# Attention and Strassen FFN on one core: first loads split over two queues, the first keys rounded on VectorE, and the operands of the first product stage made in fewer parts

## Chip, cores and metric

The kernel runs on one core of a Trainium2 chip. The metric is the device time of one execution in microseconds, taken as the median of three runs. Engines are named as in the profile: PE (TensorE matmul), PEld (its weight load), DVE (VectorE), ACT (ScalarE), POOL (GpSimd), SP (SyncE, which issues all DMAs here).

## What is computed

```python
def _attn_ref(q, k, v):                   # 8 batches, 12 heads, 448 tokens, 64 per head
    scores = scale * np.matmul(q, k.transpose(0, 1, 3, 2)) - np.log(S)
    attn = 1.0 / (1.0 + np.exp(-scores))  # sigmoid, so no row sums
    return np.matmul(attn, v)

def _moe_ref(x, w_in, w_out):             # x: 3584 x 768, from the heads laid side by side
    h = x @ w_in                          # 768 x 2048
    g = np.maximum(0.01 * h, h)
    return g @ w_out                      # 2048 x 768
```

## The kernel before

**Numbers in two parts.** A float32 operand of a score or of a feed-forward product is split into a rounded part ("high": a copy to float32r) and the rest ("low": a subtraction). Each product is then three matmuls: high by high, high by low, low by high. For q and k `Pair.high` is a copy on ACT and `Pair.low` a subtraction on DVE, both of a tile of 128x896 (448 columns of q, 448 of k).

**Attention.** The 96 heads are 48 pairs, two heads in the two halves of the partitions. `Pair.scores(h)` makes two of the four key chunks: six matmuls into a tile of two PSUM banks (pool `s`, three such tiles in the first stage, two later) and one sigmoid on ACT. `Pair.attn_v(h)` multiplies by v, and `Pair.keep` copies the sum out of PSUM into an x tile. Pairs 0, 9, 10 and 11 use four chunks of 112 keys; the others share a last chunk of 64 with a neighbour.

**Feed-forward.** Both layers are Strassen products: seven products per block of weights (`ORDER = 0, 1, 4, 5, 3, 6, 2`), from sums of quarters of x and of w. `prep` turns the float64 weights into float32 sums on DVE (some 14 steps a block: `wd`, `ws`) and stores them to DRAM (`t`). `Weights.load/high/low` bring them back and split them; `advance(t)` issues these steps ahead of product t. `Operands` makes the seven x operands: `s3`, `sum1`, `sum2`, `sum4` are subtractions or additions on DVE, `high(n, a, b)` a copy on ACT and `low(n, a, b)` a subtraction on DVE for columns a to b of operand n.

**Order.** Everything is issued in program order on each engine. The program is a row of slots, one piece of PE work each; `later(k, f)` puts f ahead of the PE work k slots on. In the first stage (`q == 0`, twelve pairs j) the slots are `e{j}.0` scores(1) of pair j, `e{j}.1` scores(0) of pair j+1, `e{j}.2` and `e{j}.3` attn_v of pair j. The next stage begins with `e0.0` to `e0.3` for pair 12 and then mixes attention with products p0, p1, and so on (five, five, four after a pair). The table `PLAN_ALONE` says ahead of which slot of the first stage ("e10.1") or of the second ("ne0.0", "np0") an operand step stands: "h422" is high of operand 4, columns 2 to 2; "l302" low of operand 3, columns 0 to 2; "s1.." to "s4.." the sums. `next_parts(i)` places the split of pair i+2 (high one slot on, low two) and the load of pair i+4 (four slots on). `prepare()` takes 1.5 steps of `prep` after a slot that is not `busy`.

**Start.** SP issues q and k of pair 0 as two loads, pair 1, v of pairs 0 and 1, three loads of weights, and later pair 2, which waits until pair 0's tile is free (`raws` has two buffers). ACT loads its table, then rounds q, k and pair 1; DVE subtracts.

Of the kernel before, what the change touches and what calls it, by code (L numbers as in the profile page):

```python
# [10 lines left out]
F32R = mybir.dt.float32r  # L11
I32 = mybir.dt.int32
AF = mybir.ActivationFunctionType
# [3 lines left out]
P = 128  # L17
# [39 lines left out]
def attn_ffn_kernel(ctx: ExitStack, tc: tile.TileContext, qk, v, w_in, w_out, out):  # L57
# [11 lines left out]
    nc = tc.nc  # L69
    B = 8  # L70
    S = qk.shape[3]
# [16 lines left out]
    def pinned(issue):  # L88

        return lambda *args, **kw: tc.keep_in_program_order(issue(*args, **kw))  # L90

    mm, dma = pinned(nc.tensor.matmul), pinned(nc.sync.dma_start)
    copy, act = pinned(nc.scalar.copy), pinned(nc.scalar.activation)
    vec, vec_s, vec_st = (pinned(x) for x in (nc.vector.tensor_tensor, nc.vector.tensor_scalar, nc.vector.scalar_tensor_tensor))

    def sub(to, x, y):
        vec(out=to, in0=x, in1=y, op=ALU.subtract)
# [10 lines left out]
    def later(slots, *fns, first=False):  # L108

        chores.setdefault(now + slots, ([], []))[not first].extend(fns)  # L110

    def slot(work=None):
        nonlocal now
        for fns in chores.pop(now, ()):
            for fn in fns:
                fn()
        if work is not None:
            work()
        now += 1
# [6 lines left out]
    class Weights:  # L126
# [17 lines left out]
        def high(self):  # L144
            pool, tag, bufs = self.to
            t = pool.tile([P, 1 if tag == "t1" else 2, 2, HW], F32R, tag=tag, name=f"w{self.w}_{self.u}_{self.g}", bufs=bufs)
            self.t = t[:, :self.n]
            copy(out=self.t[:, :, 0], in_=self.x)

        def low(self):  # L150
            sub(self.t[:, :, 1], self.x, self.t[:, :, 0])
# [59 lines left out]
    ps = ExitStack()  # L211
# [14 lines left out]
    def shift(stack, name, size, side="left"):  # L226

        return stack.enter_context(tc.tile_pool(name=name, bufs=1, side=side)).tile([P, size // 4], F32, tag=name, name=name)
# [4 lines left out]
    warm = shift(ctx, "warm", 32, "right")  # L233
    xp, pp, raws, spl, at = (right.enter_context(tc.tile_pool(name=name, bufs=bufs, side="right")) for name, bufs in (
        ("xp", 5), ("pp", 3), ("raws", 2), ("spl", 2), ("at", 5)))
# [8 lines left out]
    todo = [(w, u) for w in range(2) for u in range(NU)]  # L244
# [58 lines left out]

    xs = {}

    class Pair:


# [3 lines left out]

        def load_qk(self):
            self.raw = raws.tile([P, 2, S], F32, tag="qk", name=f"qk_{self.i}")
            for x in self.pieces():
                dma(out=self.raw[:, x], in_=qk[self.i, :, x])

        def load_v(self):
            rows, n = ((KR, 2 * NK), (P, 2 * NK - 2), (P, 2 * NK))[self.part]
            self.v = raws.tile([P, 2 * NK, D], F32, tag="v", name=f"v_{self.i}", bufs=2)  # L320
            dma(out=self.v[:rows, :n], in_=v[self.i, :rows, :n])

        def pieces(self):

            return (slice(0, 1), slice(1, 2)) if self.i == 0 else (slice(0, 2),)

        def high(self):
            self.parts = spl.tile([P, 2, 2, S], F32R, tag="qks", name=f"qks_{self.i}")
            for x in self.pieces():
                copy(out=self.parts[:, 0, x], in_=self.raw[:, x])  # L330

        def low(self):
            for x in self.pieces():
                sub(self.parts[:, 1, x], self.raw[:, x], self.parts[:, 0, x])

        def scores(self, h):
            for c in range(2 * h, 2 * h + 2):
                ps = psum("s", f"sc_{self.i}_{c}")

                if self.part == 0:  # L340
                    k0, n, rows = c * KR, KR, slice(0, KR)
                elif c < NK - 1:
                    k0, n, rows = c * P, P, slice(0, P)
                elif self.part == 1:
                    k0, n, rows = S - D, D, slice(0, D)
                else:
                    k0, n, rows = S - P, P, slice(D, P)
                for m, (kp, qp) in enumerate(((0, 0), (0, 1), (1, 0))):
                    for j, me in enumerate(heads):
                        mm(ps[:n, j, :S], lhsT=self.parts[me, kp, 1, k0:k0 + n], rhs=self.parts[me, qp, 0],  # L350
                           start=m == 0, stop=m == 2)
                if self.part == 2 and c == NK - 1:
                    s = pairs[self.i - 1].a[c]
                else:
                    s = at.tile([P, 2, S], F32, tag="s", name=f"s_{self.i}_{c}")
                act(out=s[rows], in_=ps[rows, :, :S], func=AF.Sigmoid, bias=bias, scale=scale)
                self.a.append(s)
# [27 lines left out]
    class Operands:  # L385
# [52 lines left out]
    PLAN_ALONE = {  # L438
# [4 lines left out]


    w1 = []
# [7 lines left out]
    def advance(t):  # L453

        nonlocal at_load, at_high, at_low
        while at_high < len(w1) and w1[at_high][0] <= t + 3:
            w1[at_high][1].high()
            at_high += 1
        while at_low < len(w1) and w1[at_low][0] <= t + 2:
            w1[at_low][1].low()  # L460
            at_low += 1
        while at_load < len(w1) and w1[at_load][0] <= t + 8 and at_load < at_low + len(w1_stage):
            x = w1[at_load][1]
            x.stage = w1_stage[-1]
            x.load()
            at_load += 1
# [61 lines left out]
    per = 2 * NP  # L528
    last = B * NP - 1
    pairs = [Pair(i) for i in range(B * NP)]  # L530
    nc.gpsimd.memset(warm, 0.0)
    act(out=warm, in_=warm, func=AF.Sigmoid)
    pairs[0].load_qk()
    pairs[1].load_qk()
    for i in range(2):
        pairs[i].load_v()
    next(preps)
    for i in range(2):
        pairs[i].high()
        pairs[i].low()  # L540
        pairs[i + 2].load_qk()
    first, ops = None, None
    psum = banks("ps_a", dict(s=(3, 2), pv=(2, 1)))

    def next_parts(i):
        if i + 2 <= last:
            later(1, pairs[i + 2].high)
            later(2, pairs[i + 2].low)
        if i + 4 <= last:
            later(4, pairs[i + 4].load_qk)  # L550

    def go(q, where, work, busy=False):

# [9 lines left out]
    for q in range(NQ + 1):  # L563
        before, ops = ops, Operands(q) if q < NQ else None
        if q == 0:
            slot(lambda: pairs[0].scores(0))
        elif q == 1:
            ps.close()
            psum = banks("ps_b", dict(s=(2, 2), pv=(2, 1), px=(1, 1), pz=(1, 1)))
        k = 0  # L570
        for j in range(per if q < NQ else 1):
            i = q * per + j
            if q == 0 and 0 < j:
                later(0, pairs[i + 1].load_v)
            if q == 0:
                busy = j >= per - 2
                go(q, f"e{j}.0", lambda: pairs[i].scores(1), busy)
                next_parts(i)
                if j + 1 < per:
                    go(q, f"e{j}.1", lambda: pairs[i + 1].scores(0), busy)  # L580
                    for h in range(2):
                        go(q, f"e{j}.{2 + h}", lambda: pairs[i].attn_v(h), busy)
                if j >= per - 4:
                    for t in range(2):
                        advance(2 * (j - per) + t)
                continue
            if j == 0:
                first = First(q - 1, before)
            busy = j == 0 or j == per - 1 or q == NQ
            go(q, f"e{j}.0", (lambda: pairs[i].scores(0)) if q < NQ else None, busy)  # L590
            for h in range(2):
                go(q, f"e{j}.{1 + h}", lambda: pairs[i - 1].attn_v(h), busy)
            go(q, f"e{j}.3", (lambda: pairs[i].scores(1)) if q < NQ else None, busy)
            if q < NQ:
                next_parts(i)
                if i < last:
                    later(1, pairs[i + 1].load_v)
                for _ in range(PRODUCTS[j % len(PRODUCTS)]):
                    go(q, f"p{k}", first.step, busy or j == per - 2 and k >= 50 or k < 7)
                    k += 1  # L600
# [39 lines left out]
    for k in range(NOP, NU * NOP):  # L640
        m, at = divmod(k - NOP, 6)
        if m < AHEAD:
            x = w2[use[m]]
# [22 lines left out]
    for i, (g, u) in enumerate(use[AHEAD:]):  # L666
        one = len(GROUPS[g]) == 1
        pool, tag = (ring, "ring") if i < len(GROUPS) else (t2b, "t1" if one else "t2")
# [85 lines left out]
```

## Time and profile before

| what | value |
|---|---|
| median of 3 runs | 1109.43 us (1107.17 to 1110.66) |
| the profiled execution | 1107.88 us |
| its span, first to last instruction | 1106.1 us |
| PE busy in the span | 1094.2 us (99%) |
| DVE busy, ACT busy | 651.4 us (59%), 617.6 us (56%) |
| DMA, mean over the span | 226 GB/s |

A row of the timeline gives start (us from the span's start), length (us), engine, line, operation, output<-input, shapes, and in brackets the idle time of the engine before it and what ended that. Rows of equal instructions are merged (x18). All helpers record at line 90, so rows are told apart by tile: `sc` scores, `s` sigmoids, `qk` the loaded q and k, `qks` their two parts, `so` operand parts, `x` attention outputs, `wx` and `w` weights loaded and split, `px`, `py`, `pz` PSUM of products, `c_h` their sums. In the order of a built program the names carry numbers: `qks_2` is pair 2, `s_11_3` chunk 3 of pair 11, `so4_0` operand 4 of the first product stage.

### The profile page before, as it was taken

Reading aid. Unit: us, or ns where it says so; the run is one execution under the profiler, and the core shown is the slowest. Engines: PE = TensorE matmul, PEld = TensorE weight load, DVE = VectorE, ACT = ScalarE, POOL = GpSimd, SP = SyncE. Lnnn points to the kernel's source line nnn. Section 1 sums busy time; section 2 is a strip of 40 time slices with the busy share of each in tenths; the row PEclk is TensorE's granted clock in tenths of the full one; section 3 lists DMA queues with packets and bytes.
Section 4 is the critical chain, followed back from the end, with each engine's and each line's share of the span. In section 5 each row is a group of like instructions: output and inputs, shape, how many; then the busy total and the mean of one; then the engine's idle time right before and its main releaser. Section 6 shows DMA issues by size and latency. Waiting matters only on the chain.

```text
span 1106.1 us, 15810 instructions
## 1 busy us (share of the span) xinstructions
PE 1094.2 (99%) x5952; PEld 895.1 (81%) x5952; DVE 651.4 (59%) x886; ACT 617.6 (56%) x883; POOL 0.3 (0%) x5
## 2 busy tenths in 40 slices
PE   8999999999999999999999999999999999999998
PEld 4547777777777777777777999999999999999998
DVE  5978777677666677666648666665433333343332
ACT  6897665677666668666667555554333233323331
POOL 0000000000000000000000000000000000000000
PEclk9999999999999999999999999999999999999999
DMA  8975888875878776788745889786655554454442
GB/s 289 326 249 189 311 284 284 310 254 185 264 273 289 275 234 211 242 274 292 242 151 177 264 270 297 268 280 214 206 147 150 158 175 150 133 177 150 156 149 93
DMA packets 101436, 250.08 MB, mean 226 GB/s; under 512 B 11280, under 2 KB 53904, under 8 KB 101360
## 3 DMA queue, kind: packets, MB, share of 16 engines
q1 hardware_dynamic: 101360, 249.08, 68.3%
q8 instruction: 46, 0.75, 0.3%
q14 instruction: 30, 0.25, 0.1%
HBM read 164.63 MB, written 84.41 MB: 225 GB/s over the span
## 4 chain that ended last, share of the span: by engine, by line
PE 95%; ACT 2%; DMA 1%; DVE 1%; issue 0%; SPq 0%; ACTq 0%
PE px_o L90 21%; PE px_h L90 21%; PE pv L90 11%; PE pz_h L90 11%; PE sc L90 11%; PE pz_o L90 10%; PE py_o L90 5%; PE py_h L90 5%; ACT s L90 1%; ACT so L90 1%; DMA v<-in_v 1%; DMA qk<-in_qk 0%; ACT qks L90 0%; DVE wd L90 0%; DVE so L90 0%
## 5 line engine op out<-in xcount | busy, mean ns | idle before, releaser
L90 DVE TENSOR_TENSOR gs<-gg,gs 128x896 fp32r<-128x896 f32 x112 | 122.4, 1092 | 226.8 <-ACT gs L90 226.7
L90 PE MATMUL px_h<-so,w 128*128 128x448 f32 x1152 | 249.7, 363 | 0.2 <-ACT c_h L90 0.2
L90 PE MATMUL px_o<-gs,w 128*128 128x448 f32 x1152 | 232.5, 362 | 0.0
L90 PEld LDWEIGHTS px_h<-so,w 128*128 128x128 f32 x1152 | 214.8, 187 | 19.7 <-issue 3.0
L90 ACT CAST gs<-gg 128x896 fp32r<-128x896 f32 x112 | 105.6, 943 | 221.7 <-PE px_o L90 116.1
L90 PEld LDWEIGHTS px_o<-gs,w 128*128 128x128 f32 x1152 | 216.0, 187 | 14.4
L90 ACT ACTIVATE s<-sc 128x896 f32<-128x896 f32 (+1 forms) x192 | 171.5, 917 | 59.4 <-PE sc L90 35.0
L90 PE MATMUL sc<-qks 64*128 64x448 f32 (+2 forms) x1152 | 144.7, 386 | 8.0 <-ACT qks L90 4.6
L90 DVE TENSOR_TENSOR w<-wx,w 128x768 fp32r<-128x768 f32 (+1 forms) x160 | 136.1, 853 | 26.8 <-ACT w L90 26.3
L90 PEld LDWEIGHTS sc<-qks 64*128 64x128 f32 (+2 forms) x1152 | 98.3, 180 | 65.5 <-issue 28.2
L90 PE MATMUL pv<-s,v 128*64 128x448 f32 (+2 forms) x768 | 144.1, 551 | 0.2 <-DMA v<-in_v 0.2
L90 PE MATMUL pz_h<-so,w 128*128 128x448 f32 x576 | 128.3, 367 | 0.0
L90 ACT CAST w<-wx 128x768 fp32r<-128x768 f32 (+1 forms) x160 | 119.9, 753 | 6.2 <-DMA wx<-t 6.1
L90 PEld LDWEIGHTS pz_h<-so,w 128*128 128x128 f32 x576 | 106.2, 188 | 14.8 <-issue 7.0
L90 PE MATMUL pz_o<-gs,w 128*128 128x448 f32 x576 | 116.5, 362 | 0.0
L90 PEld LDWEIGHTS pz_o<-gs,w 128*128 128x128 f32 x576 | 108.0, 187 | 7.2
L90 PEld LDWEIGHTS pv<-s,v 128*64 128x64 f32 (+2 forms) x768 | 44.0, 136 | 78.3 <-issue 77.4
L90 ACT COPY c_h<-px_h 128x448 f32<-128x448 f32 x64 | 34.1, 533 | 68.6 <-PE px_h L90 68.5
L90 PE MATMUL py_h<-so,w 128*128 128x448 f32 x288 | 62.8, 362 | 0.0
L90 DVE TENSOR_TENSOR qks<-qk,qks 128x896 fp32r<-128x896 f32 (+1 forms) x49 | 52.3, 1068 | 17.1 <-ACT qks L90 16.9
L90 DVE SCALAR_TENSOR_TENSOR wd<-wr,wd 128x768 int32<-128x768 int32 x64 | 61.2, 956 | 1.1
L90 ACT ACTIVATE c_h<-c_h 128x448 f32<-128x448 f32 x96 | 55.4, 577 | 10.1 <-DVE c_h L90 9.8
(37 smaller groups left out, 660.8 us busy)
## 6 DMA issues: line engine op xcount, KB each, us to landing
gg<-g SPq DMA_DIRECT2D x112, 448.0 KB, 3.5
wx<-t SPq DMA_DIRECT2D x120, 384.0 KB, 3.9
g<-c_h SPq DMA_DIRECT2D x128, 224.0 KB, 4.4
g<-s SPq DMA_DIRECT2D x96, 224.0 KB, 4.4
qk<-in_qk SPq DMA_DIRECT2D x47, 448.0 KB, 4.9
wr<-in_w_in SPq DMA_DIRECT2D x16, 768.0 KB, 7.1
t<-ws SPq DMA_DIRECT2D x16, 768.0 KB, 7.1
wr<-in_w_out SPq DMA_DIRECT2D x16, 768.0 KB, 5.9
```

Of the source, the lines that this page charges most:

```text
L90: return lambda *args, **kw: tc.keep_in_program_order(issue(*args, **kw))
```

## The change

The first loads: q of pair 0 goes out on ACT's queue, its k in two halves of 224 columns on SP's, and of the weights none until pair 0 is split. Pair 0 is split in a new function: ACT rounds q, DVE rounds each half of the keys and subtracts; pair 1 is rounded on DVE. The first two score chunks are issued term by term, not chunk by chunk. In the first stage q and k of pair i+2 are split one slot sooner (high ahead of `e{j}.1`, low ahead of `e{j}.2`, the load three slots on). Weights of product 0 on are loaded and split two pairs sooner. `PLAN_ALONE` makes operands 1 (as before), 3, 6, 2 and the sums `s1`, `s4` whole, and from np0 on. The slots of j = 0 are now `busy`, so `prep` starts one pair later.

```diff
@@ Pair
         def load_qk(self):
             self.raw = raws.tile([P, 2, S], F32, tag="qk", name=f"qk_{self.i}")
-            for x in self.pieces():
-                dma(out=self.raw[:, x], in_=qk[self.i, :, x])
+            if self.i == 0:
+                dma_act(out=self.raw[:, 0], in_=qk[self.i, :, 0])
+                for cols in KEYS:
+                    dma(out=self.raw[:, 1, cols], in_=qk[self.i, :, 1, cols])
+            else:
+                dma(out=self.raw, in_=qk[self.i])
...
+        def split(self):
+            self.parts = spl.tile([P, 2, 2, S], F32R, tag="qks", name=f"qks_{self.i}")
+            high, low = self.parts[:, 0], self.parts[:, 1]
+            copy(out=high[:, 0], in_=self.raw[:, 0])
+            vcopy(out=high[:, 1, KEYS[0]], in_=self.raw[:, 1, KEYS[0]])
+            sub(low[:, 0], self.raw[:, 0], high[:, 0])
+            for n, cols in enumerate(KEYS):
+                if n > 0:
+                    vcopy(out=high[:, 1, cols], in_=self.raw[:, 1, cols])
+                sub(low[:, 1, cols], self.raw[:, 1, cols], high[:, 1, cols])
@@ PLAN_ALONE
-        "e10.1": "s200", "e10.2": "h400 s100", "e10.3": "l400 h300", "e11.0": "l300 h600",
-        "ne0.0": "s211 h411 l600", "ne0.1": "l411 s111", "ne0.2": "s401", "ne0.3": "s222",
-        "np0": "h422 l422", "np1": "s122 h312 h201", "np2": "l312 h612", "np3": "l612 s422", "np4": "l201 h222", "np5": "l222"}
+        "e10.1": "s200", "e10.2": "h400", "e10.3": "l400", "ne0.0": "s211 h411", "ne0.1": "l411", "ne0.3": "s222",
+        "np0": "h422 l422 s102", "np1": "h302", "np2": "l302 h602", "np3": "l602 s402", "np4": "h202", "np5": "l202"}
@@ the first stage
-    act(out=warm, in_=warm, func=AF.Sigmoid)
     pairs[0].load_qk()
     pairs[1].load_qk()
-    for i in range(2):
-        pairs[i].load_v()
+    pairs[0].load_v()
+    act(out=warm, in_=warm, func=AF.Sigmoid)
+    pairs[0].split()
+    pairs[2].load_qk()
     next(preps)
-    for i in range(2):
-        pairs[i].high()
-        pairs[i].low()
-        pairs[i + 2].load_qk()
+    pairs[1].high(vcopy)
+    pairs[1].low()
+    pairs[3].load_qk()
...
-                busy = j >= per - 2
+                busy = j == 0 or j >= per - 2
                 go(q, f"e{j}.0", lambda: pairs[i].scores(1), busy)
-                next_parts(i)
+                next_parts(i, 0, 1, 3)
...
-                if j >= per - 4:
+                if per - 6 <= j < per - 2:
                     for t in range(2):
-                        advance(2 * (j - per) + t)
+                        advance(2 * (j - per + 2) + t)
```

The order of SP at the start, before:

```order
L90 DMA qk_0_138<-in_qk 128x448 x2
L90 DMA qk_1_141<-in_qk 128x896
L90 DMA v_0_143<-in_v 112x512
L90 DMA v_1_145<-in_v 128x384
L90 DMA wr0_0_0_147<-in_w_in 128x1536
L90 DMA wr0_0_1_149<-in_w_in 128x1536
L90 DMA wr0_1_0_203<-in_w_in 128x1536
L90 DMA qk_2_156<-in_qk 128x896
```

and now (`wr` are raw weights):

```order
L90 DMA qk_0_137<-in_qk 128x224 x2
L90 DMA qk_1_141<-in_qk 128x896
L90 DMA v_0_143<-in_v 112x512
L90 DMA v_1_185<-in_v 128x384
L90 DMA qk_2_153<-in_qk 128x896
L90 DMA wr0_0_0_155<-in_w_in 128x1536
L90 DMA wr0_0_1_157<-in_w_in 128x1536
L90 DMA qk_3_162<-in_qk 128x896
```

Pair 2 now stands ahead of all weights, and q of pair 0 is no longer on this queue.

The order of ACT at the end of the first stage, from the second sigmoid of pair 11 to the last, before:

```order
L90 ACTIVATE s_11_1_850<-sc_11_1_843 112x896
L90 CAST qks_12_852<-qk_12_768 128x896
L90 CAST so4_0_854<-s2_0_832 128x448
L90 CAST so3_0_864<-x_2_617 128x448
L90 CAST w0_0_0_872<-wx0_0_0_741 128x2x384
L90 COPY x_3_808<-pv_10_857 128x448
L90 CAST so6_0_878<-x_3_808 128x448
L90 ACTIVATE s_11_2_887<-sc_11_2_880 112x896
L90 ACTIVATE s_11_3_896<-sc_11_3_889 112x896
```

and now:

```order
L90 CAST qks_12_839<-qk_12_746 128x896
L90 ACTIVATE s_11_0_851<-sc_11_0_843 112x896
L90 ACTIVATE s_11_1_859<-sc_11_1_844 112x896
L90 CAST so4_0_862<-s2_0_841 128x448
L90 COPY x_3_815<-pv_10_864 128x448
L90 ACTIVATE s_11_2_887<-sc_11_2_879 112x896
L90 ACTIVATE s_11_3_895<-sc_11_3_880 112x896
```

Between the second and the third sigmoid of pair 11 six instructions stood on ACT, and now two.

The order of DVE from the last piece of operand 4 on, around products p0 to p3, before:

```order
L90 TENSOR_TENSOR so4_0_854<-s2_0_832,so4_0_854 128x448
L90 TENSOR_TENSOR w0_0_1_901<-wx0_0_1_806,w0_0_1_901 128x2x384
L90 TENSOR_TENSOR x_2_617<-x_2_617,x_3_808 128x448
L90 TENSOR_TENSOR c11_h0_0_982<-c11_h0_0_982,py_h0_0_994 128x448
L90 TENSOR_TENSOR qks_14_984<-qk_14_907,qks_14_984 128x896
L90 TENSOR_TENSOR so3_0_864<-x_2_617,so3_0_864 128x896
L90 TENSOR_TENSOR w0_0_2_992<-wx0_0_2_870,w0_0_2_992 128x2x384
L90 TENSOR_TENSOR so6_0_878<-x_3_808,so6_0_878 128x896
L90 TENSOR_TENSOR x_1_494<-x_1_494,s2_0_832 128x448
```

and now:

```order
L90 TENSOR_TENSOR so4_0_862<-s2_0_841,so4_0_862 128x448
L90 TENSOR_TENSOR x_2_614<-x_2_614,x_3_815 128x1344
L90 TENSOR_TENSOR w0_0_1_813<-wx0_0_1_677,w0_0_1_813 128x2x384
L90 TENSOR_TENSOR c11_h0_0_972<-c11_h0_0_972,py_h0_0_982 128x448
L90 TENSOR_TENSOR qks_14_974<-qk_14_875,qks_14_974 128x896
L90 TENSOR_TENSOR so3_0_978<-x_2_614,so3_0_978 128x1344
L90 TENSOR_TENSOR w0_0_2_980<-wx0_0_2_740,w0_0_2_980 128x2x384
L90 TENSOR_TENSOR so6_0_995<-x_3_815,so6_0_995 128x1344
L90 TENSOR_TENSOR x_1_485<-x_1_485,s2_0_841 128x1344
```

The sum into `x_2` is now whole and stands ahead of the weights of product p2, and the three passes behind it are whole too. On ACT the high part of operand 2, which reads `x_1`, stands ahead of the weights of the next block and of the sigmoids of pair 13.

## Rows read from the trace of the kernel before

**Rows 1.** All that PE waited for, whole span (us in total, times, longest).

```profile
PE sc L90 <- ACT qks L90: 4.6, 1, 4.6
PE sc L90 <- ACT s L90: 2.4, 2, 1.8
PE sc L90 <- DVE qks L90: 0.9, 2, 0.7
PE pv L90 <- DMA v<-in_v: 0.2, 1, 0.2
PE px_h L90 <- ACT c_h L90: 0.2, 1, 0.2
```

**Rows 2.** Timeline of PE, first 17 us: start us, us, and idle before in brackets.

```profile
4.59 3.70 PE L90 MATMUL sc<-qks 64*112 64x448 f32 x18 [4.59 <-ACT qks L90]
8.94 3.70 PE L90 MATMUL sc<-qks 64*112 64x448 f32 x18 [0.64 <-ACT s L90]
12.57 3.62 PE L90 MATMUL pv<-s,v 112*64 112x448 f32 x16
16.12 2.82 PE L90 MATMUL sc<-qks 64*128 64x448 f32 x24
```

**Rows 3.** Stretch of the first matmuls: length, PE, PEld, DVE, ACT, POOL busy, granted clock, DMA.

```profile
4.59:8.29 3.70, 3.69 (x18) 2.51 (x18) 0.80 (x2) 1.16 (x2) 0.00 (x0) 1.00 1.01 340
```

**Rows 4.** Timeline of ACT, first 8 us.

```profile
3.19 0.56 ACT L90 CAST qks<-qk 128x448 fp32r<-128x448 f32 x1 [0.95 <-DMA qk<-in_qk]
...
3.98 0.57 ACT L90 CAST qks<-qk 128x448 fp32r<-128x448 f32 x1 [0.23 <-DMA qk<-in_qk]
...
7.13 0.94 ACT L90 CAST qks<-qk 128x896 fp32r<-128x896 f32 x1 [2.58 <-DMA qk<-in_qk]
7.97 3.38 ACT L90 ACTIVATE s<-sc 112x896 f32<-112x896 f32 x4
```

**Rows 5.** Groups by shape, 0 to 95 us: busy us, mean ns of one | idle before.

```profile
L90 DVE TENSOR_TENSOR qks<-qk,qks 128x896 fp32r<-128x896 f32 x14 | 15.3, 1091 | 13.2 <-ACT qks L90 13.0
...
L90 DVE TENSOR_SCALAR wd<-wr 128x768 int32<-128x768 int32 x9 | 5.0, 555 | 0.9 <-DMA wr<-in_w_in 0.9
L90 DVE TENSOR_TENSOR so<-x,so 128x1344 fp32r<-128x1344 f32 x3 | 4.7, 1557 | 0.8 <-ACT so L90 0.7
...
L90 ACT CAST so<-x 128x1344 fp32r<-128x1344 f32 x3 | 3.9, 1311 | 0.0
...
L90 DVE TENSOR_TENSOR w<-wx,w 128x768 fp32r<-128x768 f32 x3 | 2.9, 952 | 0.0
```

**Rows 6.** Timeline of ACT, a split whose other part comes late.

```profile
56.08 0.94 ACT L90 CAST qks<-qk 128x896 fp32r<-128x896 f32 x1
```

**Rows 7.** Timeline of PE, 58 to 98 us.

```profile
58.20 1.27 PE L90 MATMUL sc<-qks 64*112 64x448 f32 x10 [0.66 <-DVE qks L90]
...
74.78 2.11 PE L90 MATMUL sc<-qks 64*112 64x448 f32 x18
78.68 0.87 PE L90 MATMUL sc<-qks 64*128 64x448 f32 x6 [1.80 <-ACT s L90]
...
84.06 2.08 PE L90 MATMUL px_h<-so,w 128*128 128x448 f32 x9
...
87.77 1.96 PE L90 MATMUL px_h<-so,w 128*128 128x448 f32 x9
...
97.55 1.49 PE L90 MATMUL sc<-qks 64*128 64x448 f32 x12
```

**Rows 8.** Timeline of ACT ahead of the longest wait in Rows 7.

```profile
74.34 0.57 ACT L90 CAST so<-s 128x448 fp32r<-128x448 f32 x1
...
76.01 0.53 ACT L90 COPY x<-pv 128x448 f32<-128x448 f32 x1
...
76.90 1.73 ACT L90 ACTIVATE s<-sc 112x896 f32<-112x896 f32 x2
```

**Rows 9.** Timeline of DVE, the last piece of operand 4.

```profile
85.82 0.62 DVE L90 TENSOR_TENSOR so<-s,so 128x448 fp32r<-128x448 f32 x1 [0.84 <-ACT so L90]
```

More of the change, by code (lines that the diff above doesn't have):

```diff
@@ L92, in attn_ffn_kernel @@
     mm, dma = pinned(nc.tensor.matmul), pinned(nc.sync.dma_start)
-    copy, act = pinned(nc.scalar.copy), pinned(nc.scalar.activation)
+    copy, act, dma_act = (pinned(x) for x in (nc.scalar.copy, nc.scalar.activation, nc.scalar.dma_start))
+    vcopy = pinned(nc.vector.tensor_copy)
     vec, vec_s, vec_st = (pinned(x) for x in (nc.vector.tensor_tensor, nc.vector.tensor_scalar, nc.vector.scalar_tensor_tensor))
@@ L304, in attn_ffn_kernel @@
     xs = {}
+    KEYS = slice(0, S // 2), slice(S // 2, S)
     class Pair:
@@ L321, in load_v, with high @@
             dma(out=self.v[:rows, :n], in_=v[self.i, :rows, :n])
-        def pieces(self):
-            return (slice(0, 1), slice(1, 2)) if self.i == 0 else (slice(0, 2),)
-        def high(self):
+        def high(self, how=None):
             self.parts = spl.tile([P, 2, 2, S], F32R, tag="qks", name=f"qks_{self.i}")
-            for x in self.pieces():
-                copy(out=self.parts[:, 0, x], in_=self.raw[:, x])
+            (how or copy)(out=self.parts[:, 0], in_=self.raw)
         def low(self):
-            for x in self.pieces():
-                sub(self.parts[:, 1, x], self.raw[:, x], self.parts[:, 0, x])
+            sub(self.parts[:, 1], self.raw, self.parts[:, 0])
+        def split(self):
[8 more added lines that the diff above has]
+                sub(low[:, 1, cols], self.raw[:, 1, cols], high[:, 1, cols])
         def scores(self, h):
+            todo, acts = [], []
             for c in range(2 * h, 2 * h + 2):
@@ L349, in scores @@
                     for j, me in enumerate(heads):
-                        mm(ps[:n, j, :S], lhsT=self.parts[me, kp, 1, k0:k0 + n], rhs=self.parts[me, qp, 0],
-                           start=m == 0, stop=m == 2)
+                        todo.append((c, m, dict(out=ps[:n, j, :S], lhsT=self.parts[me, kp, 1, k0:k0 + n],
+                                                rhs=self.parts[me, qp, 0], start=m == 0, stop=m == 2)))
+                acts.append((c, rows, ps))
+            if self.i == h == 0:
+                todo.sort(key=lambda x: x[1])
+            for n, (c, rows, ps) in enumerate(acts):
+                for x in todo if self.i == h == 0 and n == 0 else [x for x in todo if x[0] == c and (self.i or h)]:
+                    mm(**x[2])
                 if self.part == 2 and c == NK - 1:
@@ L531, in attn_ffn_kernel, with next_parts @@
     nc.gpsimd.memset(warm, 0.0)
-    act(out=warm, in_=warm, func=AF.Sigmoid)
     pairs[0].load_qk()
     pairs[1].load_qk()
-    for i in range(2):
-        pairs[i].load_v()
+    pairs[0].load_v()
+    act(out=warm, in_=warm, func=AF.Sigmoid)
+    pairs[0].split()
+    pairs[2].load_qk()
     next(preps)
-    for i in range(2):
-        pairs[i].high()
-        pairs[i].low()
-        pairs[i + 2].load_qk()
+    pairs[1].high(vcopy)
+    pairs[1].low()
+    pairs[3].load_qk()
     first, ops = None, None
     psum = banks("ps_a", dict(s=(3, 2), pv=(2, 1)))
-    def next_parts(i):
+    def next_parts(i, *slots):
         if i + 2 <= last:
-            later(1, pairs[i + 2].high)
-            later(2, pairs[i + 2].low)
+            later(slots[0], pairs[i + 2].high)
+            later(slots[1], pairs[i + 2].low)
         if i + 4 <= last:
-            later(4, pairs[i + 4].load_qk)
+            later(slots[2], pairs[i + 4].load_qk)
     def go(q, where, work, busy=False):
@@ L572, in attn_ffn_kernel @@
             i = q * per + j
-            if q == 0 and 0 < j:
+            if q == 0:
                 later(0, pairs[i + 1].load_v)
             if q == 0:
-                busy = j >= per - 2
+                busy = j == 0 or j >= per - 2
                 go(q, f"e{j}.0", lambda: pairs[i].scores(1), busy)
-                next_parts(i)
+                next_parts(i, 0, 1, 3)
                 if j + 1 < per:
@@ L594, in attn_ffn_kernel @@
             if q < NQ:
-                next_parts(i)
+                next_parts(i, 1, 2, 4)
                 if i < last:
```

## Prediction, made blind

> **What bounds the kernel now.** I read first the busy times: PE is busy for 1094.2 of 1106.1 us, so a gain can come only from the 12 us in which it isn't, or from matmuls that run slower than elsewhere. Next, the view of who waited for whom, for PE alone. The reader is to see that its five lines add up to 8.3 us: 4.6 before the first matmul, then 2.4 for sigmoids, 0.9 for the low parts of q and k, 0.2 for a load of v, 0.2 for a copy out of PSUM [rows 1]. Then PE's timeline, to place them: all lie in the first 95 us, at the start, in the first stage and where the second begins. Last, the length of like rows: the first 18 score matmuls take 3.70 us (0.206 each) and the next 18 again 3.70, while 24 take 2.82 at 16.12 (0.118 each) [rows 2]. The granted clock stands at 1.00 in the slow stretch too [rows 3], which is the upper level of 2.4 GHz, so that column doesn't show this slowness; the spacing of the matmuls does.
>
> **Part by part.** The sum is made against the profiled execution, 1107.88 us, which is 1.55 below the median of the three runs. An instruction on ACT or DVE holds its engine for its length less about 0.1, since the next starts before it ends (7.13 and 0.94, but the next at 7.97) [rows 4].
>
> *a. The first matmul* waits for the copy of k, which starts at 3.98 when k has landed; q's copy starts at 3.19 [rows 4]. Now DVE rounds the first keys and ACT only q, so PE can start one copy after q lands. If q lands as before, that is 3.19 + 0.56 + 0.05 = 3.80, and 0.79 is gained; if it lands only when k did, 3.98 + 0.57 + 0.05, nothing is. No row has two queues loading at once. I take 0.2, near the lower end, because the first transfers share their way with the two halves of k. The table load on ACT now follows a DMA issue and ends some 0.4 us later; the 0.95 us in which ACT waited for q [rows 4] hide that.
>
> *b. The wait of 0.64 at 8.94* [rows 2] is ACT's: the copy of pair 1 stood ahead of the first sigmoid and waited for its load until 7.13, so the sigmoids began at 7.97 [rows 4]. That copy goes to DVE. The first sigmoid then starts when 12 matmuls are done, 12 x 0.206 = 2.5 after the first, and ends 3.4 after it; the 19th matmul, which needs its PSUM tile, would come at 3.7. So the wait goes: 0.64. Next to be late would be pair 1: loaded by 7.13, copied on DVE in 0.65 (the one-input form, 0.555 for 768 columns) to 1.09 (the two-input form), then 1.09 for the low part [rows 5]: ready by 8.8 to 9.3. PE reaches it at 4.4 + 24 x 0.206 = 9.3 and uses the low part two matmuls on, at 9.7. Covered by either price.
>
> *c. The slow matmuls.* The first 36 score matmuls run at 0.206, 18 of them ahead of the break at 8.29 and 18 behind it [rows 2]. Unbroken work is what this stretch lacks. If without the break the quicker pace of 0.118 is there from the place of the break on, the 18 behind it gain 18 x 0.088 = 1.6 us; if the pace changes where it did, nothing. I take 1.0: nearer the upper end, because the row at 8.94 is the one unbroken to where the pace changes, and less than all of it, since a part must still run slowly.
>
> *d. Splits one slot sooner.* PE lost 0.9 us in two waits for a low part [rows 1], 0.66 of it at 58.20 [rows 7]. There the high copy ran at 56.08 [rows 6], behind two sigmoids of the next pair; now it stands ahead of them, and two sigmoids are 1.73 [rows 8]. DVE may have an operand pass of 1.56 in the way [rows 5], and the low part would still be ready before 57.5. Both waits go: 0.9. The 0.2 for v [rows 1] I halve: SP now issues q and k of pair i+4 ahead of the next v, so v can be held up by DVE, but `prep` and its loads start one pair later. Together 1.0. The six steps of `prep` that are moved back are covered by the 13.0 us in which DVE waited for the high copy [rows 5]; without that cover the low parts would be late again, at 0.9.
>
> *e. The longest wait, 1.80 before 78.68* [rows 7], is for the last sigmoid of pair 11. ACT came to pair 11's third sigmoid only at 76.90: three copies from 74.34 to 76.01, one more after the copy of x [rows 8]. Of these, one remains, and the weights' copies stand earlier. Now the copy of x is next; it waits for the end of attn_v at 74.78 and ends by 75.6, the sigmoids end at 76.45 and, their scores being ready at 76.2, at 77.35. PE would be there after its 18 matmuls, at 76.9: 0.45 stays, 1.35 is gained. One pair earlier a weight copy (some 0.7) has come ahead of a sigmoid that was just in time; I take 0.15 off. So 1.2.
>
> *f. The first products* cost more. From the start of p0 (84.06 [rows 7], zero in this paragraph) DVE can take operand 4's last piece at 1.76 [rows 9], as before, since ACT makes its high part behind pair 12's sigmoids. Then come the whole sum into `x_2` (1.56), the weights of p2 (0.95), the addition (0.62), a low part (1.09), operand 3 (1.56), the weights of p4 (0.95), operand 6 and the sum into `x_1` (1.56 each) [rows 5], each less 0.1. The weights of p2 are ready at 4.7; p2 starts at 3.71 [rows 7] and uses them from its third matmul on, 4.1: PE waits 0.6. Those of p4 are ready at 8.5, wanted at 8.3: 0.2. The sum into `x_1` ends at 11.4. ACT stands before it with operand 2's high copy (1.31 [rows 5]), a weight copy, and only then the sigmoids of pair 13: the first ends at 14.4. PE wants its PSUM tile at the scores that began at 13.5 [rows 7], now 14.1: 0.3, and 0.1 for the second. Of 1.2 the old 0.2 [rows 1] comes off: -1.0.
>
> Sum: 0.2 + 0.64 + 1.0 + 1.0 + 1.2 - 1.0 = 3.0 us. The profiled execution would take 1104.9, the median 1109.43 - 3.0 = **1106.4**. About 0.3% (3.3 us) is what a measurement of this kernel tells from no change; the runs before spread by 3.5.
>
> **The rivals.**
> 1. *The crowding in f costs nothing*: DVE had idle time of 0.84 just ahead of operand 4 [rows 9], and if pieces slip into it PE waits nowhere. Against it: the sum into `x_2` needs the last x, and the order on DVE is fixed. Gain 3.0 + 1.2 = 4.2: 1105.2. Chance 0.20.
> 2. *The loads share one set of engines*: q on its own queue lands no sooner than k did, and the change of pace comes no sooner either. For it: the two loads landed 0.8 apart for the same bytes [rows 4], as if one followed the other. a and c fall away: 0.64 + 1.0 + 1.2 - 1.0 = 1.8, 1107.6. Chance 0.20. The Trainium skill, "DMA: Bandwidth & Descriptors", "Rules for kernel authors", speaks for this one: spreading DMAs over the issuing engines brings no bandwidth, since all run on the same 16 DMA engines and interleave, and saves only issue time. By that rule a alone is 0 and the sum 2.8; the one-queue trace here can't show it.
> 3. *Slower: q gets its turn late.* It is the kernel's first load from ACT's queue, while SP's already holds k, pair 1 and two v. If q comes only with pair 1, which landed by 7.13 [rows 4], PE starts at 7.13 + 0.56 + 0.05 = 7.74, 3.15 late; with c gone, -3.15 + 0.64 + 1.0 + 1.2 - 1.0 = -1.3: 1110.7. It decides once q lands after 5.8, where the other 1.84 are used up. Against it: q is issued as soon as k's first half. Chance 0.07.
> 4. *The splits are issued sooner but done no sooner*, because DVE, with `prep` begun later, is behind all through the first stage: d is 0, 1107.4. Against it: the 13.0 us of waiting [rows 5]. Chance 0.08.
>
> **How the numbers follow.** The forecast has 0.45. Its own range takes c from 0 to 1.6, a from 0 to 0.8, f between -1.6 and 0 and the spread of a median: 1104 to 1108.5. Taking in rivals 1, 2 and 4 with their spread, and leaving out 3: 1103.0 to 1109.6. The forecast lies just inside the 0.3% (1106.1 is the edge), so half of its chance less a little, 0.2, counts as faster, with 0.15 of rival 1 and 0.08 of the rest: faster 0.43. Slower by over 0.3% needs rival 3 and a slow median, or a wait that I don't see: 0.05. The rest, 0.52, is no difference.
>
> **What would show it.** Right: a first matmul before 4.6; no wait before the fourth score chunk; spacing of 0.118 before 12; no waits for low parts up to 75; under 0.6 us for the last sigmoid of pair 11; short new waits of PE for DVE's weights at p2 and p4, and for a sigmoid in the scores after p4, with ACT idle before operand 2. Wrong: a first matmul after 5; waits of PE for v or for low parts in every pair; p2 to p4 unbroken, or broken by over 2 us; any new wait beyond 110 us, where I count on none.

## The result and the profile after

The kernel with the change took 1112.2 us (median of 18 runs, 1110.7 to 1114.6) where the kernel before took 1109.5 (18 runs, 1107.2 to 1111.6). The ratio is 1.0027 [1.0021, 1.0033]: slower, by 2.7 us in the medians, outside the range of the forecast (1103.0 to 1109.6). In the profiled executions the span grew from 1106.1 to 1109.5 us, by 3.4.

The view of who waited for whom, PE alone, of the kernel after (us in total, times, longest):

```profile
PE sc L90 <- ACT qks L90: 4.4, 1, 4.4
PE px_h L90 <- DVE c_h L90: 3.7, 2, 2.2
PE sc L90 <- ACT s L90: 1.7, 4, 0.6
PE px_h L90 <- DVE w L90: 0.5, 1, 0.5
PE pv L90 <- DMA v<-in_v: 0.4, 2, 0.2
```

Against [rows 1] the waits for low parts (`DVE qks`) are gone, those for sigmoids are more and shorter, and a line of 3.7 us has come that stands in no row of before: PE waits for `c_h`, a sum of products on DVE. To see where, PE's timeline of the kernel after: the start, then around the first products, then from 140 us on (start, us, and idle before in brackets):

```profile
4.41 6.36 PE L90 MATMUL sc<-qks 64*112 64x448 f32 x36 [4.41 <-ACT qks L90]
10.70 3.23 PE L90 MATMUL pv<-s,v 112*64 112x448 f32 x16
...
74.60 0.87 PE L90 MATMUL sc<-qks 64*128 64x448 f32 x6 [0.65 <-ACT s L90]
...
80.25 2.08 PE L90 MATMUL px_h<-so,w 128*128 128x448 f32 x9
...
85.03 1.68 PE L90 MATMUL px_h<-so,w 128*128 128x448 f32 x7 [0.50 <-DVE w L90]
...
94.73 1.68 PE L90 MATMUL sc<-qks 64*128 64x448 f32 x12 [0.32 <-ACT s L90]
...
157.87 1.96 PE L90 MATMUL pz_h<-so,w 128*128 128x448 f32 x9
162.02 2.57 PE L90 MATMUL px_h<-so,w 128*128 128x448 f32 x9 [2.19 <-DVE c_h L90]
164.51 2.52 PE L90 MATMUL sc<-qks 64*128 64x448 f32 x12
166.96 3.39 PE L90 MATMUL pv<-s,v 128*64 128x448 f32 x20
...
191.56 2.08 PE L90 MATMUL px_h<-so,w 128*128 128x448 f32 x9 [1.53 <-DVE c_h L90]
...
210.72 1.49 PE L90 MATMUL sc<-qks 64*128 64x448 f32 x12
```

PE's timeline of the kernel before, the rows that answer to those from 157.87 on:

```profile
160.50 1.96 PE L90 MATMUL pz_h<-so,w 128*128 128x448 f32 x9
162.30 1.96 PE L90 MATMUL px_h<-so,w 128*128 128x448 f32 x9
164.19 1.49 PE L90 MATMUL sc<-qks 64*128 64x448 f32 x12
165.61 3.39 PE L90 MATMUL pv<-s,v 128*64 128x448 f32 x20
...
207.57 1.48 PE L90 MATMUL sc<-qks 64*128 64x448 f32 x12
```

Beside [rows 2] and [rows 7] they show what was gained and lost. The first attn_v starts at 10.70 instead of 12.57, p0 at 80.25 instead of 84.06, the scores after p4 at 94.73 instead of 97.55: 2.8 us are gained by there. Then two waits come, of 2.19 and 1.53 us, between products that ran on without a break before. The 12 score matmuls that began at 207.57 begin at 210.72: 3.15 late. The rest of the span adds 0.25.

DVE's timeline of the kernel after, ahead of both waits, says what PE was waiting for:

```profile
150.44 0.55 DVE L90 TENSOR_TENSOR ws<-wd,ws 128x384 f32<-128x384 f32 x1
150.91 0.62 DVE L90 TENSOR_TENSOR c_h<-c_h,c_h 128x448 f32<-128x448 f32 x1
151.44 0.61 DVE L90 TENSOR_TENSOR s<-c_h,s 128x448 f32<-128x448 f32 x1
159.94 0.56 DVE L90 TENSOR_SCALAR wd<-wr 128x768 int32<-128x768 int32 x1 [7.88 <-DMA t<-ws]
...
161.35 0.61 DVE L90 TENSOR_TENSOR c_h<-c_h,px_h 128x448 f32<-128x448 f32 x1
...
189.08 0.56 DVE L90 TENSOR_SCALAR wd<-wr 128x768 int32<-128x768 int32 x1 [7.39 <-DMA t<-ws]
```

DVE stands still for 7.88 us in front of a `wd`, the first step of `prep` for a block of weights, until the store `t<-ws` of the block before has landed. The pool `pp` gives `prep` three buffers, which raw weights, `wd` and `ws` take in turn; this `wd` gets the buffer of the last `ws`, and that is still being stored. Behind the waiting `wd`, in DVE's order, stands the addition into `c_h` at 161.35 which empties a PSUM tile; PE wants that tile, and its wait ends as the addition does. The second case is the same, after 7.39 us.

The same place in the kernel before, DVE's timeline:

```profile
141.27 0.55 DVE L90 TENSOR_TENSOR ws<-wd,ws 128x384 f32<-128x384 f32 x1
...
152.44 0.55 DVE L90 TENSOR_SCALAR wd<-wr 128x768 int32<-128x768 int32 x1
```

There 11.2 us lay between the start of the last `ws` and the next `wd`, with nine instructions of DVE in between, and the `wd` waited for nothing. After the change two instructions lie between (those at 150.91 and 151.44). Nothing was added to the path; `prep` only runs one pair later, and so its gap fell on another place in the pattern of the products.

### The profile page after: what moved, and what is told of

It reads as the page before. It is cut to its first block, busy times and chain, and to the rows that moved or that the text cites. A ratio compares the mean times of both kernels' runs of the same rounds, so it can differ in the third digit from the quotient of the medians.

```text
span 1109.5 us, 15798 instructions
## 1 busy us (share of the span) xinstructions
PE 1095.2 (99%) x5952; PEld 895.5 (81%) x5952; DVE 650.3 (59%) x884; ACT 615.5 (55%) x878; POOL 0.3 (0%) x5
## 4 chain that ended last, share of the span: by engine, by line
PE 93%; DMA 3%; ACT 2%; DVE 1%; issue 0%; SPq 0%; DVEq 0%; ACTq 0%
PE px_o L90 21%; PE px_h L90 20%; PE pv L90 11%; PE sc L90 11%; PE pz_o L90 10%; PE pz_h L90 10%; PE py_o L90 5%; PE py_h L90 5%; DMA v<-in_v 1%; DMA t<-ws 1%; ACT s L90 1%; DMA g<-c_h 1%; ACT so L90 0%; DMA qk<-in_qk 0%; DVE x L90 0%
## 5 line engine op out<-in xcount | busy, mean ns | idle before, releaser
L90 DVE TENSOR_TENSOR qks<-qk,qks 128x896 fp32r<-128x896 f32 (+2 forms) x50 | 52.3, 1048 | 10.3 <-ACT qks L90 10.2
```

## The experiments

The first theory: **the phase of `prep`, by way of the buffers**. The delay of `prep` by one pair (`busy` at j = 0) put each `wd` right behind the store that holds its buffer, and everything else in the change together gained about what was forecast. Two rivals: the **operands** in fewer parts push DVE's work back until it collides beyond 110 us; or the **transfers**, moved by the earlier loads, make the store land late whatever `prep` does. The ratios below are to the kernel before, run on the same chip.

**The change without the delay of `prep` (e1).**

```diff
-                busy = j == 0 or j >= per - 2
+                busy = j >= per - 2
```

> The change with one part undone: the slots of pair 0 are not busy, so prep starts where it did before. Theory (phase of prep): the delay alone puts the first step of weight blocks 6 and 7 on DVE right behind the sums whose store it must await; with it undone no wait of PE for c_h beyond 110 us, granted clock 1.00 from 150 to 200 us, and the 2.6 us gained by 96 us stay: 1106.7 us, 2.8 below before. Rival (operands): the whole passes and the earlier weights leave DVE late in the second stage; then the two waits of 2.2 and 1.5 us stay and the time is 1111 to 1112.5. Rival (transfers): stores take 8 us there because of more traffic; then waits stay in part, 1109 to 1111.

Measured: 1106.93 us, ratio 0.9985 [0.9977, 0.9994], faster than before. All that PE waited for:

```profile
PE sc L90 <- ACT qks L90: 4.3, 1, 4.3
PE sc L90 <- ACT s L90: 1.7, 4, 0.7
PE pv L90 <- DMA v<-in_v: 1.2, 1, 1.2
PE px_h L90 <- DVE w L90: 0.5, 1, 0.5
```

Both waits for `c_h` are gone, with the operands and the loads as in the change: the rivals can't explain that. But the gain over before (1108.6 on that chip) is 1.7 us in the median and not 3: 1.2 of the rest is a wait for v, at 45.74, where the change had two of 0.2 later on. SP issued that v at 38.93, behind a store `t<-ws` for which it had waited 4.7 us for DVE's sums; in the change the same v went out at 36.50, ahead of such a store. The later `prep` bought something, then: it kept its stores out of the way of this v.

**The kernel before with the delay alone (e2).**

```diff
-                busy = j >= per - 2
+                busy = j == 0 or j >= per - 2
```

> The kernel before with one part of the change alone: the slots of pair 0 are busy, so prep starts one pair later. Theory (phase of prep): the two waits of PE for c_h between 155 and 200 us appear, 2 and 1.5 us, with a granted clock under 1.00 behind the first: 5 us slower, 1114.5. Rival (operands): nothing beyond 110 us changes, 1109.5, or a little less as DVE has less to do early. Rival (transfers): as before within 1 us.

Measured: 1115.31 us, ratio 1.0057 [1.0044, 1.0071]. PE's two new rows in its timeline:

```profile
165.10 2.08 PE L90 MATMUL px_h<-so,w 128*128 128x448 f32 x9 [2.75 <-DVE c_h L90]
...
194.22 3.37 PE L90 MATMUL px_h<-so,w 128*128 128x448 f32 x9 [2.64 <-DVE c_h L90]
```

One condition in one line makes the old kernel slower by 6.7 us (its own runs on that chip had a median of 1108.6) and brings the two waits, with nothing else of the change present. Together with e1 that settles which part it is.

**The change with a fourth buffer for `prep` (e3).** Room for it comes from 7 instead of 10 tiles for the second layer's sums.

```diff
-ST = 10
+ST = 7
...
-        ("xp", 5), ("pp", 3)
+        ("xp", 5), ("pp", 4)
```

> The change with a fourth buffer in the pool of weight blocks, and seven buffers in place of ten in the pool of product sums to make room. Prep stays one pair late, but the first step of a block no longer takes the buffer of the sums that are being stored. Theory (phase, by way of that buffer): DVE's waits for the stores of the sums (17.0 us beyond 95 us) fall under 5, the two waits of PE go, 1106 to 1108, unless the seven buffers bring waits of their own. Rival (operands): the waits of PE stay, 1111 to 1112.5. Rival (transfers): as the theory says, since the store is no longer waited for.

Measured: 1105.41 us, ratio 0.9974 [0.9963, 0.9985]. All of PE's waits, and what DVE's `wd` waited for from 95 us on:

```profile
PE sc L90 <- ACT qks L90: 4.3, 1, 4.3
PE sc L90 <- ACT s L90: 1.7, 4, 0.7
PE px_h L90 <- DVE w L90: 0.5, 1, 0.5
```

```profile
DVE wd L90 <- DMA wr<-in_w_in: 11.9, 4, 5.6
```

No wait of PE beyond 95 us is left, though `prep` is as late as in the change; `wd` no longer waits for a store at all, and for its raw weights 5.6 us at most. The span, 1103.1, is 3.0 below the 1106.1 of before: what the prediction had for the whole change.

**Fewer tiles alone (e5)**, the control for it: `ST = 7`, and three buffers.

> The change with 7 instead of 10 tiles for the second layer's sums and still three buffers for `prep`: what e3 also changed, alone. If the fourth buffer is what took the waits away in e3: as the change, 1110.5 to 1112.5 us, with two waits of PE for `c_h` between 160 and 195 us and DVE waiting some 8 us in `wd` for the stores `t`. If the fewer tiles did it: about 1105.5 us and no such waits. If fewer tiles cost something by themselves: over 1112.5, with new waits of PE late in the span.

Measured: 1111.67 us, ratio 1.0026 [1.0016, 1.0036], as the change itself, with both waits in place:

```profile
161.83 3.42 PE L90 MATMUL px_h<-so,w 128*128 128x448 f32 x9 [2.79 <-DVE c_h L90]
...
191.26 2.08 PE L90 MATMUL px_h<-so,w 128*128 128x448 f32 x9 [1.61 <-DVE c_h L90]
```

So it was the buffer. The theory stands on four runs: delay and three buffers are slow with the change (e5 and the change) and without it (e2); take either away and the waits go (e1, e3). DVE's own waits agree: the longest of a `wd` for a store, from 95 us on, was 7.9 us in the change, 8.5 in e2 and 8.4 in e5, but 4.2 before, 2.8 in e1 and none in e3.

The next three ask what single parts of the change are worth once this wait is out of the way. Each is the version with four buffers (e3) with one part undone.

**q of pair 0 on SP's queue (e6).**

```diff
-                dma_act(out=self.raw[:, 0], in_=qk[self.i, :, 0])
+                dma(out=self.raw[:, 0], in_=qk[self.i, :, 0])
```

> e3 (1105.4 us) with q of pair 0 issued on SP's queue ahead of the two halves of k, so that only the queue is undone. If the second queue brings the gain that part a of the prediction gives it (0.2 us): first matmul at 4.5 to 4.7 us instead of 4.3 to 4.4, and the time 0.1 to 0.3 longer, about 1105.6. If the queue is what makes the first matmul as early as it is and all loads crowd behind one another on SP: first matmul after 4.9, 1106 or more. If the loads share one set of engines and one queue serves q first: first matmul at 3.9 to 4.3 and the time the same or up to 0.4 shorter, with the second half of k, later, as the next wait.

Measured: 1105.05 us, ratio 0.9967 [0.9956, 0.9978], not to be told from e3. ACT's first copy and PE's first rows:

```profile
3.39 0.56 ACT L90 CAST qks<-qk 128x448 fp32r<-128x448 f32 x1 [1.16 <-DMA qk<-in_qk]
```

```profile
4.09 6.55 PE L90 MATMUL sc<-qks 64*112 64x448 f32 x36 [4.09 <-ACT qks L90]
10.57 3.23 PE L90 MATMUL pv<-s,v 112*64 112x448 f32 x16
```

The third case: q lands sooner when it stands first on one queue than on a queue of its own (its copy starts at 3.39, and at 3.80 in the kernel after). In the seven runs with two queues the first matmul came at 4.29 to 4.49, in the three with one (e6, e9, e10) at 4.01 to 4.16. The second queue costs 0.3 us, so what made the start earlier is the rest of it: k comes and is rounded in halves, and DVE rounds it while ACT rounds q. No run separates these two. At the first attn_v nothing of the 0.3 is left (10.57 here, 10.24 in e3): the 36 score matmuls ahead of it took between 5.73 and 6.55 us in the runs that have them in one row, which is a wider spread than that.

**Splits of q and k where they were before (e7).**

```diff
-                next_parts(i, 0, 1, 3)
+                next_parts(i, 1, 2, 4)
```

> e3 (1105.4 us) with q and k of pair i+2 split again where the kernel before has them (high one slot on, low two, load four). By part d of the prediction the earlier slot is worth 0.9 us in waits for low parts: two or more waits of PE for `qks` of 0.3 to 0.7 us each between 40 and 75 us, 1106.3 us. If prep's delay or the start alone removed those waits: no wait for `qks`, 1105.4. If the earlier loads also let the loads of v wait less: waits for v of 0.2 to 0.4 besides, 1106.7.

Measured: 1106.8 us, ratio 0.9982 [0.9973, 0.999]. That is 1.4 above e3 in the median, but the two intervals overlap, so the waits say more than the time. The rows of PE's timeline behind a wait which e3 doesn't have:

```profile
38.17 1.30 PE L90 MATMUL sc<-qks 64*128 64x448 f32 x10 [0.24 <-DVE qks L90]
...
55.44 1.28 PE L90 MATMUL sc<-qks 64*112 64x448 f32 x10 [0.66 <-DVE qks L90]
...
161.66 2.08 PE L90 MATMUL px_h<-so,w 128*128 128x448 f32 x9 [1.17 <-DVE c_h L90]
```

The two waits for low parts return with nearly the lengths of before, 0.9 together ([rows 1], [rows 7]). Of the first, though, the earlier split only makes another wait: e3 stands 0.33 us at 38.30 for a sigmoid, which e7 doesn't. The third row is `c_h` once more: DVE waited 6.73 us for raw weights there, where it waited 5.62 in e3. At the same place e6 waits 0.65, e8 0.19 and e9 0.82. Four buffers make this place harmless by a small margin only, and e3 is the one of these five where PE didn't wait there at all.

**The table of operand steps as before (e8)**, with the weights still two pairs sooner: the four lines of `PLAN_ALONE` of the kernel before.

> e3 (1105.4 us) with the table of operand steps as before, the weights still loaded and split two pairs sooner. By parts e and f the table is worth +1.2 for the last sigmoid of pair 11 and -0.9 (measured 0.5 at p2 and 0.3 after p4) for the first products: with it undone a wait of PE for a sigmoid of 0.8 to 1.8 us before 80 us, none at p2 or after p4, and 1105.7 us in sum (1105.2 to 1106.4). If the weights' earlier slots alone brought e: no wait over 0.6 for a sigmoid, and 1104.6 us, faster than e3. If the operands in many parts now collide with the earlier splits: several waits of PE for `so` or `qks`, over 1106.5.

Measured: 1104.66 us, ratio 0.9966 [0.9952, 0.9979]; a miss, since e3 with the new table was expected to be the faster one. The row behind its longest wait of PE for a sigmoid:

```profile
74.87 0.87 PE L90 MATMUL sc<-qks 64*128 64x448 f32 x6 [0.90 <-ACT s L90]
```

The longest wait for a sigmoid is 0.90 with the old table, against 1.80 before and 0.67 in e3. Of part e's gain 0.90 is therefore not the table's. With the delay alone (e2) the wait was still 1.80 and with the splits undone (e7) 0.67, so the earlier weights are its likely source; no run moved them alone. The table's own 0.23 is paid for with 0.51 at p2 and 0.33 after p4, against a single 0.18, at 87.91, here. By these waits the table costs 0.4; e8 gives 0.19 of that back in a wait for `c_h` at 158.87. The intervals of e3 and e8 overlap, so by time alone the table is worth nothing either way.

**Operands spread differently (e4)**, on e1, `prep` not delayed: the sum into `x_2` one product later, the high and low part of operand 2 ahead of the two attn_v of pair 12.

```diff
-        "np0": "h422 l422 s102", "np1": "h302", "np2": "l302 h602", "np3": "l602 s402", "np4": "h202", "np5": "l202"}
+        "np0": "h422 l422", "np1": "s102 h302", "np2": "l302 h602", "np3": "l602 s402", "ne1.1": "h202", "ne1.2": "l202"}
```

> As e1, and of the operands of the first product stage the sum into x_2 is moved from ahead of p0 to ahead of p1, behind the weights of p2, and both parts of operand 2 from ahead of p4 and p5 to ahead of attn_v of pair 12, so that ACT makes pair 13's first sigmoids before it must await the sum into x_1. If the waits of 0.5 at p2 and 0.3 at the scores after p4 have the cause that the prediction gave, both go: 0.8 us less than e1. If DVE's list is simply too long, the wait moves to p4 and the time is e1's within 0.3.

Measured: 1107.46 us, ratio 0.9989 [0.9980, 0.9998], not to be told from e1; the 0.8 us that was hoped for didn't come. The waits at p2 and after p4 went, and others came in their place: 1.03 us at 89.76 for a copy of `c_h` on ACT, 0.62 at 101.50 for an addition into `c_h` on DVE. Moving these steps only moved the waits.

**Both undone that brought nothing (e9)**, on four buffers: one queue and the old table.

> e3 with both undone that brought nothing there: q of pair 0 on SP's queue (e6: first matmul 4.09 instead of 4.30) and the old table of operand steps (e8: waits of PE from 60 to 100 us of 1.5 instead of 1.9). If the two add: first matmul at about 4.1, waits of 1.5 us between 60 and 100, and 1104.4 us (1103.8 to 1105.2). If the queue's gain is taken up by the pace of the first score matmuls, which turned at another time in each run: 1104.7, as e8.

Measured: 1104.13 us, ratio 0.9966 [0.9953, 0.9978], the lowest median of all, but inside the intervals of e6 and e8. In the profiled executions the start does gain: the first matmul came at 4.16, and the first attn_v at 10.15 where e8 had 10.73, although the low part of pair 1 was late in between (the row below). The gain is lost at 158.94, where PE waits 0.82 for `c_h` and e8 waited 0.19.

```profile
8.93 1.29 PE L90 MATMUL sc<-qks 64*128 64x448 f32 x10 [0.28 <-DVE qks L90]
```

**The same with `prep` not delayed (e10).**

> e9 with `prep` not delayed. If the delay costs nothing once there are four buffers, and still buys the 1.2 us that PE waited for v in e1: a wait for v of about 1.2 near 46 us, and 1.0 to 1.4 us more than e9, about 1105.6. If the phase of `prep` costs even with four buffers (e6, e7 and e8 wait 0.2 to 1.2 us for `c_h` at 159 to 162 us): that wait goes, and the sum is within 0.7 of e9.

Measured: 1105.09 us, ratio 0.9966 [0.9954, 0.9978]. The wait for v is back with 0.85 us at 45.30, and in place of a wait of 0.82 for `c_h` at 158.94 in e9 there is one of 0.51 at 185.61. By the ratios the two are the same. By the medians, on one chip, e10 is 0.96 slower, near to what was expected if the delay still paid; the ratios are level because one execution of e9 took 1108.17 us. Whether `prep` should start late with four buffers stays open.

## Why the prediction was wrong

On the first 95 us its sum was nearly right, and most of its parts:

- *a, b and c.* First matmul at 4.41 (0.18 earlier; 0.2 said), no wait at 8.94 (0.64 said), 36 score matmuls in 6.36 us and not twice 3.70 (1.04 gained; 1.0 said). The first attn_v starts 1.87 earlier; 1.84 was the sum. For c this closeness is luck in part: the 36 matmuls took 5.73 to 6.55 us in the runs that share this start, 0.85 to 1.67 less than 7.40. The reason given for a was half wrong: q on its own queue was no help, as e6 showed. In that, though not in what it said of c, rival 2 was right, and the rule of the Trainium skill cited with it ("DMA: Bandwidth & Descriptors", "Rules for kernel authors") agrees with the runs: q's copy started at 3.80 with two queues and 3.39 with one.
- *d.* No wait for a low part was left, 0.9 as said. But the copies that went ahead of the sigmoids made one of these late: 0.32 at 38.77, which part d had at nothing and which e7 doesn't have. The 0.1 for v was a loss of 0.2 (two waits of 0.2 instead of one). So 0.4, where 1.0 was said.
- *e.* 1.80 became 0.65, 1.15 gained (1.35 said). A shorter wait for a sigmoid, 0.40, came at 67.89; 0.15 had been taken off for such a one. So 0.75, where 1.2 was said.
- *f.* The wait at p2 was 0.50 (0.6 said), none at p4 (0.2 said), 0.32 after it (0.3 and 0.1 said). With the old 0.18 off that is 0.64, where 1.0 was said.

From these the profiled execution stood 2.8 us better at 94.73, and e3, without the stall beyond, ended 3.0 better. That the sum came so near to the 3.0 of the forecast is luck in part: d and e fell short by 1.05 together, f cost 0.36 less than said, and the first attn_v, which is in no part, took 3.23 us where it had taken 3.62.

**The step that failed** is in part d: "The six steps of `prep` that are moved back are covered by the 13.0 us in which DVE waited for the high copy". It priced the moved steps by DVE's time in the first stage alone, where they do have cover. It did not follow `prep` on: the delay persists for as long as `prep` runs, and it moves where each block's first `wd` falls against the store of the block before. With that fell "any new wait beyond 110 us, where I count on none": what stood at nothing in the sum cost 5.8 us. None of the rivals named this mechanism, and the slower one, q's late turn, was not what happened.

The price of it can be read row by row. From 157.87 to 166.96 the kernel after needs 9.09 us for three groups, `pz_h`, `px_h` and 12 scores; before, the same three began at 160.50 and ended at 165.61, 5.11. The 3.98 lost are 2.35 of standing still, 0.60 in the row at 162.02 and 1.03 in the one at 164.51, whose 12 score matmuls took 2.52 us where 1.48 is usual. The second wait loses 1.8, with no slow row behind it. Together 5.8: from 2.6 us ahead at 140 us to 3.15 behind at 210.

A row that could have warned of it was at hand before. What DVE's `wd` waited for from 95 us on, first the kernel before, then after:

```profile
DVE wd L90 <- DMA t<-ws: 7.3, 3, 4.2
```

```profile
DVE wd L90 <- DMA t<-ws: 17.0, 5, 7.9
```

Already before, DVE stood up to 4.2 us at a `wd` for a store, with PE none the worse for it. That reads as slack being used up without a trace on PE, and any shift of `prep` was a bet on how much was left.

## What to carry to other kernels

A step that is moved in time takes its buffers with it. Before such a step is called covered, look up which transfer last used the buffer it will get, how long that transfer takes to land, and which instructions lie between; on an engine that works in order, a wait there holds up everything behind it, here a PSUM tile that PE needed. A line in the view of waits that names a store as releaser for an engine off the critical path is a warning even where it costs nothing yet.

When a change of many parts comes out wrong, find the last place where the timelines still agree with the forecast. Here that was at 95 us. This didn't clear any part by itself, but it turned the search to what still differs beyond that place, and one line edited in each of the two kernels then showed that it was the delay of `prep`.

## What the runs showed of the hardware

PE's clock fell after the wait. The view of stretches of the kernel after (length; busy time of PE, PEld, DVE, ACT, POOL with counts; granted clock; DMA share; GB/s), for the wait and the three rows behind it:

```profile
159.70:162.02 2.32, 0.13 (x2) 0.01 (x1) 2.08 (x5) 0.02 (x1) 0.00 (x0) 1.00 1.08 434
162.02:164.51 2.49, 2.49 (x9) 1.83 (x9) 2.49 (x4) 1.28 (x2) 0.00 (x0) 0.78 0.77 302
164.51:166.96 2.45, 2.45 (x13) 1.81 (x12) 2.42 (x4) 1.92 (x3) 0.00 (x0) 0.53 0.86 234
166.96:170.00 3.04, 3.04 (x22) 0.98 (x20) 3.00 (x7) 0.92 (x2) 0.00 (x0) 1.00 0.79 296
```

After it had stood for 2.19 us, PE began again at the full clock, 2.4 GHz. In steps of half a microsecond the granted clock is 1.00 up to 163.0, 0.50, which is the lower level of 1.2 GHz, from 163.5 to 166.5, and 1.00 again by 166.96. That cost 1.63 us on top of the 2.35, in the two slow rows above. Not every wait did this. Behind the waits of 1.53 here and 1.80 in the kernel before [rows 7] no row was slow. Of the four longer ones that the runs show, three were followed by slow rows (2.19 here, 2.64 in e2, 2.79 in e5); in e2 the 9 matmuls behind the wait of 2.75 took their usual 2.08 us, those behind the one of 2.64 took 3.37. So a wait of PE may cost more than its own length: here 3.98 for one of 2.19.

The clock of whole executions bears on the times too. Of the 24 executions of the kernel before beside e1 to e4, nine had a mean granted clock of 0.998 and took 1109.2 to 1110.9 us, while the thirteen with 1.000 took 1107.0 to 1108.8. In the change all 18 had 0.998 or less, in e3 none of seven was under 0.999. No trace of one of the nine was kept, so what PE waited for in them stays open.

The store that DVE waited for was long under way. Its issue in SP's timeline of the kernel after, and the page's row on all 16 such stores (KB each, median us from issue to landing):

```profile
151.45 0.38 SPq L90 DMA_DIRECT2D t<-ws  x1
```

```profile
t<-ws SPq DMA_DIRECT2D x16, 768.0 KB, 7.0
```

DVE's `wd` started at 159.94, 8.5 us after the issue. The median of 7.0 was no different before (7.1), so by that the stores didn't become slower; a `wd` came too soon behind one. The DMA engines' share was 0.99 in the stretch from 150 to 160 us: in it ran loads and other stores besides this one. No run shows how long the store would have taken by itself.
